# Linear attention, a Fourier mixer and an MLP on one core: k and q of the next chunk are turned between a chunk's output products and the turning back of that output

## The chip, the core and the metric

The kernel runs on one core of a Trainium2 chip. The core has a matrix engine (TensorE, PE in the profile; its weight loads are the row PEld), a vector engine (VectorE, DVE), a scalar engine (ScalarE, ACT), GpSimd (POOL) and SyncE (SP), which here issues DMAs only. Each engine works through its own list of instructions in order, and engines wait for each other by semaphores. The metric is device time in microseconds for one execution; the median of several runs counts.

## What is computed

A decayed linear attention over 4 batches, 8 heads, 768 positions and head size 64, then a mixer on rows of 512: the real part of a Fourier transform over positions and features is added, the sum is normalised, and an MLP of width 2048 is added to it.

```python
# attention, per block of 64 positions, with D[i,j] = lam**(i-j) for i >= j
out    = (q k^T * D) v + (q * lam**(i+1)) state
state  = lam**64 * state + (k * lam**(63-i))^T v
# mixer, on x = (batch, 768, 512)
u  = x + real(fft(fft(x, axis=1), axis=2))
un = (u - mean(u)) / sqrt(var(u) + 1e-6)
y  = u + maximum(un @ w_ch1, 0) @ w_ch2
```

The MLP's weights are given in float64, all else in float32; the computation is in float32.

## The kernel before

**Attention.** `attn_chunk(b, c)` does a chunk of 128 positions of batch b for all 8 heads, six chunks to a batch. SP loads k, q and v of the chunk (L243, two buffers each). GpSimd makes kd, the decayed k (L250, one buffer). PE turns k (L254, four 128x128 transposes) and q (L259, four more) into PSUM; ACT copies them out as kT (L256) and qT (L261); for c > 0 DVE makes the decayed qs from the same PSUM bank (L264). PE forms the scores (L272); DVE multiplies them by the decay in two halves (L276, called sc). PE forms the state's increment from kd and v (L287), which DVE adds (L292, or copies in the first chunk, L289) after GpSimd has decayed the old state (L291). The output is the sum of qs times the old state (L300) and sc times v (L304) in one PSUM bank. ACT copies it to oT (L307), PE turns it back (L311), ACT copies the result to x in two halves (L314, L315), and ACT's queue stores x to memory for the mirror (L318 to L322).

**Fourier part.** The transform uses that x can be folded with its own mirror image. `mirror_a` (called by chunk 4) and `mirror_b` (by chunk 5) read mirrored rows by GpSimd's indirect DMAs (L358, L361, L366). `fft_ln(b)` folds on DVE (L347 to L396, `fold_a` and `fold_b`), transforms over positions on PE (L420), over features (L433 to L438), and adds the result on ACT and DVE (L495 to L503). `norm` does the statistics (L450, L451), a power on GpSimd (L454, L455), and the scaling (L467); for the first four groups of rows PE turns the result (L472), for the others DVE does in squares of 32 (L477) and it waits in memory.

**MLP.** Weights come in 32 pieces (L209), which DVE and ACT unpack from float64 (L214 to L222). The first four groups of rows go through a plain MLP (L535, L549) while attention and transform of later batches run. The other eight go through `late`, seven products in place of eight (L617, L664), after all attention is done.

**What sets the order.** Each stage is a Python generator that yields its rough cost; `weave` and `part` take turns between attention and Fourier part of a batch on one side and weights or MLP on the other. From this order a scheduler makes the list of each engine; it keeps dependencies and buffers and may move an instruction forward or back by some places. PSUM for all but the plain MLP is one pool of five banks (`pa`).

The sections of a run are chosen by sums of costs, a chunk being 7.3:

```python
run(weave(attn(0), part(w, 0.5 * NW), 0.5 * NW / t_att))
run(weave(part(fr, t_chunk), part(w, 0.1 * NW), 0.1 * NW / t_chunk))
```

Of the kernel before, what the change touches and what calls it, by code (L numbers as in the profile page):

```python
# [76 lines left out]
def kernel(  # L77
# [15 lines left out]
    NC = S // C  # L93
# [45 lines left out]
    def new(pool, shape, tag, **kw):  # L139
        cnt[0] += 1  # L140
        return pool.tile(shape, F32, tag=tag, name=f"{tag}{cnt[0]}", **kw)

    def psum_a(shape):
        return new(pa, shape, "pa")
# [48 lines left out]
    def load_tables(i):  # L193
        if i == 1:
            nc.sync.dma_start(cs, cn["cs"].ap())
            nc.sync.dma_start(ix, cn["ix"].ap())
        elif i == 2:
            nc.sync.dma_start(dt, cn["dt"].ap())
# [37 lines left out]
    def pair(t, hp):  # L236
        return t[:, 2 * hp:2 * hp + 2, :].rearrange("p a d -> p (a d)")

    def attn_chunk(b, c):
        rows = slice(c * C, (c + 1) * C)  # L240
        kt, qt, vt = (new(ld, [C, H, D], nm) for nm in ("k", "q", "v"))
        for t, src in ((kt, k), (qt, q), (vt, v)):
            nc.sync.dma_start(t, src[b, :, rows, :].rearrange("h p d -> p h d"))  # L243
        if b == 0:
            load_tables(c)

        last = c == NC - 1
        if not last:
            kd = new(at, [C, H, D], "kd")
            nc.gpsimd.tensor_tensor(kd, kt, kpow, op=ALU.mult)  # L250

        ptk = psum_a([128, HP, C])
        for hp in range(HP):
            nc.tensor.transpose(ptk[:, hp, :], pair(kt, hp), ident)  # L254
        kT = new(at, [128, HP, C], "kT", bufs=2)
        nc.scalar.copy(kT, ptk)  # L256
        ptq = psum_a([128, HP, C])
        for hp in range(HP):
            nc.tensor.transpose(ptq[:, hp, :], pair(qt, hp), ident)  # L259
        qT = new(at, [128, HP, C], "qT", bufs=2)  # L260
        nc.scalar.copy(qT, ptq)  # L261
        if c > 0:
            qs = new(at, [128, HP, C], "qs")
            nc.vector.tensor_tensor(qs, ptq, qpow, op=ALU.mult)  # L264
        yield 1.2


        mm = nc.tensor.matmul
        pss = [psum_a([C, HP, C]) for _ in range(2)]
        for hp in range(HP):  # L270
            for hi in range(2):
                mm(pss[hi][:, hp, :], lhsT=kT[HD[hi], hp, :], rhs=qT[HD[hi], hp, :], start=True, stop=True)  # L272
        sc = []
        for hi in range(2):
            t = new(at, [C, HP, C], "sc", bufs=3)
            nc.vector.tensor_tensor(t, pss[hi], decay[:, hi::2, :], op=ALU.mult)  # L276
            sc.append(t)
        yield 1.5


        s_old, s_new = st[(c + 1) % 2], st[c % 2]
        if not last:
            pu = psum_a([128, HP, D])
            for hp in range(HP):
                for hi in range(2):
                    h = 2 * hp + hi
                    mm(pu[HD[hi], hp, :], lhsT=kd[:, h, :], rhs=vt[:, h, :], start=True, stop=True)  # L287
            if c == 0:
                nc.vector.tensor_copy(s_new, pu)  # L289
            else:  # L290
                nc.gpsimd.tensor_tensor(s_new, s_old, spow.broadcast_to([128, HP, D]), op=ALU.mult)  # L291
                nc.vector.tensor_tensor(s_new, s_new, pu, op=ALU.add)  # L292
            yield 0.9


        po = psum_a([128, HP, C])
        if c > 0:
            for hp in range(HP):
                for hi in range(2):
                    mm(po[HD[hi], hp, :], lhsT=s_old[HD[hi], hp, :], rhs=qs[HD[hi], hp, :],  # L300
                       start=(hp == 0), stop=False, skip_group_check=True)
        for hp in range(HP):
            for hi in range(2):
                mm(po[HD[hi], hp, :], lhsT=vt[:, 2 * hp + hi, :], rhs=sc[hi][:, hp, :],  # L304
                   start=(c == 0 and hp == 0), stop=(hp == HP - 1), skip_group_check=True)
        oT = new(at, [128, HP, C], "oT")
        nc.scalar.copy(oT, po)  # L307
        yield 2.0
        px = psum_a([C, HP, 128])
        for hp in range(HP):  # L310
            nc.tensor.transpose(px[:, hp, :], oT[:, hp, :], ident)  # L311
        px = px.rearrange("p h e -> p (h e)")
        x = xn_[b, c] = new(xp, [C, DM], "x") if c < HC else new(xn, [C, DM], "xn")
        nc.scalar.copy(x[:, 0:HM], px[:, 0:HM])  # L314
        nc.scalar.copy(x[:, HM:DM], px[:, DM - 1:HM - 1:-1])  # L315
        if c == 0:
            xd[b] = (dram.tile([S - 256, DM], F32, name=f"xa{b}"), dram.tile([257, DM], F32, name=f"xb{b}"))
            nc.scalar.dma_start(xd[b][1][256:257], x[0:1])  # L318
        elif c < NC - 1:
            nc.scalar.dma_start(xd[b][0][(c - 1) * C:c * C], x)  # L320
        if c >= NC - 2:
            nc.scalar.dma_start(xd[b][1][(c - NC + 2) * C:(c - NC + 3) * C], x)  # L322
        if c == NC - 2:
            mirror_a(b)
        elif c == NC - 1:
            mirror_b(b)
        yield 1.7
# [24 lines left out]
    def mirror_a(b):  # L352

        xa = xd[b][0]

        eo[b] = [(new(fp, [128, 2, 2 * W], f"fe{a}"), new(fp, [128, 2, 2 * W], f"fo{a}")) for a in range(2)]
        for a, n in enumerate(BLK):
            gather(out=eo[b][a][1][0:n, 1, 0:DM], out_offset=None, in_=xa[:, :], in_offset=row_of(a, n))  # L358
        for t in range(2, HC):
            u = xs[b, HC + t] = new(xp, [128, DM], "x")  # L360
            gather(out=u[:, :], out_offset=None, in_=xa[:, :], in_offset=row_of(2 + t))  # L361

    def mirror_b(b):
        for t in range(2):
            u = xs[b, HC + t] = new(xp, [128, DM], "x")
            gather(out=u[:, :], out_offset=None, in_=xd[b][1][:, :], in_offset=row_of(2 + t))  # L366
        for t in range(HC):
            xs[b, t] = xn_.pop((b, t))
# [325 lines left out]
            store(*who[1], y[1], lo if s == 0 else slice(0, DM))  # L694


    def attn(b):
        for c in range(NC):
            yield from attn_chunk(b, c)

    def front(b):
        yield from attn(b)
        yield from fft_ln(b)
# [32 lines left out]
    t_att, t_front = NC * t_chunk, NC * t_chunk + 10.0 + 7.0 + 5.7 + 3 * 2.4  # L736
    t_mlp = FO * 1.7 + G * 4 * 3.4
    run(weave(attn(0), part(w, 0.5 * NW), 0.5 * NW / t_att))

    fr, mix = chain(front(b) for b in range(1, B)), fft_ln(0)  # L740
# [58 lines left out]
```

## Time and profile before

| what | us |
|---|---|
| median of 5 runs | 867.81 |
| lowest and highest run | 866.45, 870.26 |
| the profiled execution, its own time | 871.22 |
| its span, first to last instruction | 869.4 |
| PE busy, matmuls | 808.2 |
| DVE busy | 438.5 |
| ACT busy | 177.1 |
| POOL busy | 85.0 |

The profile describes one execution, whose own time is 3.4 us over the median. The span is what its instructions cover; 1.8 us lie around it. PE's busy time is the sum of its matmuls with modelled ends, so 93% busy doesn't mean 93% of its peak. Where the prediction gives a wait in square brackets, it is the idle time of that engine just before the instruction, and whose result ended it. In the view of busy time by stage each row is a stretch of the span; the figure in round brackets is a count of instructions.

### The profile page before, as it was taken

To read this page: it belongs to the slowest core of one execution; us is meant where nothing else is said; L and a number is where in the kernel's file an instruction comes from. 1 tells how busy PE (TensorE), PEld (TensorE's weight loads), DVE (VectorE), ACT (ScalarE), POOL (GpSimd) and SP (SyncE) were. 2 spreads that over 40 slices of the span, in tenths; PEclk is the share of its full clock that TensorE was granted. 3 is DMA by queue.
4 is the path that set the end of the run, shared out by engine and by line. 5 is a ranking of instruction groups with operands and counts; after the bars stand their busy time and mean duration, and the time that the engine had idled before them with its cause. 6 is when DMAs were issued, how large, how long until landed. Compare 5 with 4: busy or idle time off the path is not lost.

```text
span 869.4 us, 11653 instructions
## 1 busy us (share of the span) xinstructions
PE 808.2 (93%) x4592; PEld 645.7 (74%) x4592; DVE 438.5 (50%) x1018; ACT 177.1 (20%) x417; POOL 85.0 (10%) x107
## 2 busy tenths in 40 slices
PE   5866768899999999999999999999999999999998
PEld 4655656645877477864874888888888888888887
DVE  6768869944552438426596553125511553035411
ACT  3453325510223112220200220012100220012100
POOL 2223211100021102111000000000000000000000
PEclk9985979999999999999999999999999999999999
DMA  9897516810156405542152101110111000110010
GB/s 247 207 254 209 143 57 172 261 45 25 49 124 132 140 25 141 103 109 79 48 169 51 49 1 49 48 49 1 49 46 45 7 1 1 48 49 1 1 37 24
DMA packets 127933, 71.63 MB, mean 82 GB/s; under 512 B 111336, under 2 KB 112360, under 8 KB 127880
## 3 DMA queue, kind: packets, MB, share of 16 engines
q1 hardware_dynamic: 121920, 56.72, 25.3%
q0 software_dynamic: 2496, 7.87, 2.8%
q10 hardware_dynamic: 3464, 6.30, 2.0%
q8 instruction: 36, 0.59, 0.3%
q14 instruction: 17, 0.14, 0.1%
HBM read 49.90 MB, written 20.98 MB: 82 GB/s over the span
## 4 chain that ended last, share of the span: by engine, by line
PE 75%; DVE 9%; DMA 7%; issue 5%; ACT 2%; POOL 1%; SPq 0%; ACTq 0%; POOLq 0%; DVEq 0%
PE p L664 22%; PE p L617 22%; PE pm L535 8%; PE pm L549 8%; DMA raw<-in_moe_w_ch_dram 4%; PE pa L420 3%; PE pa L304 3%; PE pa L272 2%; PE pa L300 2%; DMA fo<-xa,ix 1%; PE pa L311 1%; DMA x<-xb,ix 1%; PE pa L287 1%; DVE w L221 1%; PE pa L254 1%
## 5 line engine op out<-in xcount | busy, mean ns | idle before, releaser
L535 PE MATMUL pm<-ut,w 128*128 128x256 f32 x512 | 122.9, 389 | 4.3 <-ACT hr L543 4.3
L549 PE MATMUL pm<-w,hr 128*128 128x512 f32 x256 | 114.8, 596 | 0.0
L535 PEld LDWEIGHTS pm<-ut,w 128*128 128x128 f32 x512 | 95.1, 193 | 21.2 <-ACT hr L543 5.5
L617 PE MATMUL p<-ur,w 128*128 128x256 f32 x384 | 93.5, 379 | 0.0
L549 PEld LDWEIGHTS pm<-w,hr 128*128 128x128 f32 x256 | 47.0, 190 | 51.8 <-issue 51.2
L617 PEld LDWEIGHTS p<-ur,w 128*128 128x128 f32 x384 | 73.0, 190 | 10.3 <-issue 0.5
L617 PE MATMUL p<-us,w1s 128*128 128x256 f32 x256 | 65.5, 379 | 0.0
L664 PE MATMUL p<-w,hs 128*128 128x256 f32 x256 | 58.0, 379 | 0.5 <-DVE y L685 0.5
L664 PE MATMUL p<-w,ha 128*128 128x256 f32 x256 | 57.9, 379 | 0.0
L664 PE MATMUL p<-w2s,hs 128*128 128x256 f32 x256 | 57.9, 379 | 0.0
L664 PEld LDWEIGHTS p<-w,hs 128*128 128x128 f32 x256 | 48.5, 190 | 7.5 <-DVE y L685 0.9
L664 PEld LDWEIGHTS p<-w2s,hs 128*128 128x128 f32 x256 | 48.7, 190 | 6.6
L664 PEld LDWEIGHTS p<-w,ha 128*128 128x128 f32 x256 | 48.7, 190 | 6.6
L617 PEld LDWEIGHTS p<-us,w1s 128*128 128x128 f32 x256 | 48.7, 190 | 6.6
L525 POOL DMA_INDIRECT out_dram<-y,ix x12 | 11.8, 981 | 404.7 <-DVE y L690 344.1
L644 ACT COPY ha<-p 128x256 f32<-128x256 f32 x32 | 11.9, 372 | 170.8 <-PE p L617 170.8
L272 PE MATMUL pa<-qT,kT 64*128 64x128 f32 x384 | 32.1, 310 | 12.0 <-ACT qT L261 12.0
L272 PEld LDWEIGHTS pa<-qT,kT 64*128 64x128 f32 x384 | 26.9, 210 | 21.4 <-ACT qT L261 19.1
L304 PE MATMUL pa<-sc,v 128*64 128x128 f32 x384 | 33.1, 299 | 9.1 <-DVE sc L276 9.1
L264 DVE TENSOR_TENSOR qs<-pa,qpow 128x512 f32<-128x512 f32 x20 | 13.8, 689 | 48.4 <-ACT qT L261 48.4
L304 PEld LDWEIGHTS pa<-sc,v 128*64 128x64 f32 x384 | 24.7, 147 | 17.1 <-DVE sc L276 12.5
L655 DVE TENSOR_TENSOR ha<-p,ha 128x256 f32<-128x256 f32 x32 | 13.6, 425 | 44.2 <-ACT ha L654 44.2
(134 smaller groups left out, 1154.1 us busy)
## 6 DMA issues: line engine op xcount, KB each, us to landing
raw<-in_moe_w_ch_dram SPq DMA_DIRECT2D x32, 512.0 KB, 5.3
k<-in_k_dram SPq DMA_DIRECT2D x24, 256.0 KB, 5.1
q<-in_q_dram SPq DMA_DIRECT2D x24, 256.0 KB, 6.4
v<-in_v_dram SPq DMA_DIRECT2D x24, 256.0 KB, 3.8
ud<-x SPq DMA_DIRECT2D x16, 256.0 KB, 2.3
utd<-uq SPq DMA_DIRECT2D x64, 64.0 KB, 2.2
ur<-utd SPq DMA_DIRECT2D x8, 512.0 KB, 4.4
u<-ud SPq DMA_DIRECT2D x16, 256.0 KB, 2.7
```

The lines of the kernel that those rows point to most:

```text
L264: nc.vector.tensor_tensor(qs, ptq, qpow, op=ALU.mult)
L272: mm(pss[hi][:, hp, :], lhsT=kT[HD[hi], hp, :], rhs=qT[HD[hi], hp, :], start=True, stop=True)
L300: mm(po[HD[hi], hp, :], lhsT=s_old[HD[hi], hp, :], rhs=qs[HD[hi], hp, :], start=(hp == 0), stop=False, skip_group_check=True)
L304: mm(po[HD[hi], hp, :], lhsT=vt[:, 2 * hp + hi, :], rhs=sc[hi][:, hp, :], start=(c == 0 and hp == 0), stop=(hp == HP - 1), skip_group_chec ...
L420: mm = nc.tensor.matmul(ps[0:m, n, :], lhsT=piece(a, i, n), rhs=cs[0:rows, a, i in (2, 3), n, :], start=(a == 0), stop=(a == 1))
L525: nc.gpsimd.indirect_dma_start(out=out.rearrange("b s d -> (b s) d"), out_offset=row_of(2 + HC * (b + 1) + T - HC), in_=y[:, :], in_offset ...
L535: nc.tensor.matmul(ps, lhsT=w1[:, c, 128 * fc:128 * fc + 128], rhs=ut[:, c, :], start=(c == 0), stop=(c == KO - 1))
L549: nc.tensor.matmul(ps, lhsT=hr[fc // 4][:, fc % 4, 128 * i:128 * i + 128], rhs=w2[:, fc, :], start=(fc == 0), stop=(fc == FO - 1))
L617: nc.tensor.matmul(ps, lhsT=s2.A[a][:, kt, 128 * i:128 * i + 128], rhs=U[b][:, kt, :], start=(first and kt == 0), stop=(kt == 1), skip_gro ...
L644: nc.scalar.copy(a11, two(X))
L655: V.tensor_tensor(a22, two(Z), a22, op=ADD)
L664: nc.tensor.matmul(ps, lhsT=h[a][:, s, i, :], rhs=s2.B[b][:, i, :], start=(first and i == 0), stop=(i == HF - 1), skip_group_check=True)
```

## The change

`attn_chunk` is cut in two. `attn_in` loads a chunk, makes kd, turns k and q and copies them out. `attn_out` does all the rest. `attn` starts the first chunk's `attn_in` and then hands each `attn_out` the `attn_in` of the next chunk, which it runs to its end after the oT copy and in front of the turning back. The last chunk of a batch gets nothing to run, and the first chunk of the next batch starts as before. The sum of the yields stays the same; the 1.2 of a chunk's input part is yielded one chunk earlier. All buffers keep their sizes. Line numbers in the text are those of the kernel before.

```diff
-    def attn_chunk(b, c):
+    def attn(b):
+
+        head = attn_in(b, 0)
+        for c in range(NC):
+            yield from head
+            head = attn_in(b, c + 1) if c < NC - 1 else ()
+            yield from attn_out(b, c, head)
+
+    ins = {}
+
+    def attn_in(b, c):
         rows = slice(c * C, (c + 1) * C)
         kt, qt, vt = (new(ld, [C, H, D], nm) for nm in ("k", "q", "v"))
...
-        last = c == NC - 1
-        if not last:
+        kd = None
+        if c < NC - 1:
             kd = new(at, [C, H, D], "kd")
             nc.gpsimd.tensor_tensor(kd, kt, kpow, op=ALU.mult)
 
...
             nc.tensor.transpose(ptq[:, hp, :], pair(qt, hp), ident)
         qT = new(at, [128, HP, C], "qT", bufs=2)
         nc.scalar.copy(qT, ptq)
+        qs = None
         if c > 0:
             qs = new(at, [128, HP, C], "qs")
             nc.vector.tensor_tensor(qs, ptq, qpow, op=ALU.mult)
+        ins[b, c] = kT, qT, qs, kd, vt
         yield 1.2
+
+    def attn_out(b, c, head):
+        kT, qT, qs, kd, vt = ins.pop((b, c))
+        last = c == NC - 1
 
...
         oT = new(at, [128, HP, C], "oT")
         nc.scalar.copy(oT, po)
         yield 2.0
+        yield from head
         px = psum_a([C, HP, 128])
         for hp in range(HP):
             nc.tensor.transpose(px[:, hp, :], oT[:, hp, :], ident)
...
-    def attn(b):
-        for c in range(NC):
-            yield from attn_chunk(b, c)
-
     def front(b):
         yield from attn(b)
         yield from fft_ln(b)
```

## The prediction

> **What bounds the kernel now.** I read the page's slices first, then busy time by stage, then who PE waited for before 97 us, then one chunk boundary in order of time.
>
> ```profile
> span 869.4 us, 11653 instructions
> PE   5866768899999999999999999999999999999998
> DVE  6768869944552438426596553125511553035411
> PEclk9985979999999999999999999999999999999999
> DMA  9897516810156405542152101110111000110010
> ...
> core 0: us, PE busy (x) PEld busy (x) DVE busy (x) ACT busy (x) POOL busy (x), PEclk, DMA share, GB/s
> 0.00:25.00 25.00, 14.99 (x112) 12.39 (x114) 16.34 (x36) 8.28 (x14) 6.95 (x19) 1.00 0.99 245
> 25.00:60.00 35.00, 23.92 (x312) 19.35 (x308) 26.11 (x48) 17.80 (x35) 5.63 (x8) 0.99 0.86 227
> 60.00:97.00 37.00, 24.01 (x208) 20.35 (x210) 30.74 (x64) 12.06 (x25) 14.47 (x11) 0.64 0.65 188
> 97.00:121.00 24.00, 17.76 (x124) 15.05 (x120) 14.44 (x34) 9.08 (x22) 3.37 (x4) 0.79 0.42 132
> 121.00:177.00 56.00, 47.00 (x329) 38.02 (x329) 51.14 (x115) 28.84 (x57) 7.92 (x10) 0.97 0.60 176
> 177.00:449.00 272.00, 263.65 (x1654) 186.18 (x1654) 136.25 (x309) 52.69 (x137) 37.96 (x50) 1.00 0.36 89
> 449.00:869.00 420.00, 416.82 (x1867) 354.34 (x1865) 163.47 (x419) 48.37 (x129) 8.74 (x9) 1.00 0.11 32
> ...
> PE pa L272 <- ACT qT L261: 10.8, 9, 3.3
> PE pa L304 <- DVE sc L276: 7.7, 6, 3.8
> PE pa L311 <- ACT oT L307: 5.6, 8, 0.8
> PE pa L300 <- DVE qs L264: 5.1, 1, 5.1
> ...
> 33.65 0.58 ACT L307 COPY oT<-pa 128x512 f32<-128x512 f32 x1 [2.86 <-PE pa L304]
> 34.28 0.66 PE L311 MATMUL pa<-ident,oT 128*128 128x128 f32 x4 [0.68 <-ACT oT L307]
> 34.78 0.60 PE L254 MATMUL pa<-ident,k 128*128 128x128 f32 x4
> 35.21 0.60 PE L259 MATMUL pa<-ident,q 128*128 128x128 f32 x4
> 36.04 0.58 ACT L261 COPY qT<-pa 128x512 f32<-128x512 f32 x1
> 36.66 0.68 DVE L264 TENSOR_TENSOR qs<-pa,qpow 128x512 f32<-128x512 f32 x1
> 36.67 1.16 PE L272 MATMUL pa<-qT,kT 64*128 64x128 f32 x16 [0.86 <-ACT qT L261]
> ```
>
> From 177 us PE is the bound: 680.5 of 692 us busy, the last 420 us with no attention in them. Before that PE has 127.7 of 177 us of work and is idle for 49. Three things hold it there. To 60 us the DMA engines are nearly full (share 0.99, 0.86) and PE stops at every chunk boundary. From 60 to 97 us DVE (30.7 of 37) folds batch 0 for its transform. From 121 to 177 us DVE (51.1 of 56) unpacks the MLP weights, and PE's MLP waits behind it in DVE's order. So a microsecond saved on PE before 177 us counts only as far as it brings DVE to the weight work earlier; after 177 us it counts at once.
>
> **What the Trainium skill says.** "TensorE: Matmul & The Clock Gate", Part 2, step 1: weight loads can be pulled ahead, "The MATMULs themselves stay in program order". The boundary above agrees: k's transposes at 34.78, long ready, stand behind L311, which waits for oT. So their place in PE's order is the whole change. The same page, Part 1: the array runs at half clock until it has been busy for some microseconds. The trace agrees: four k transposes take 1.06 us at 18.1 us and 0.60 at 34.8. "PSUM — Partial Sum Buffer", on bank collisions: two engines may not touch one bank and quadrant together, so software must order them. The trace agrees: qs starts at 36.66, when ACT's qT copy of the same bank ends (36.62). "Trainium Kernel Development and Optimization", Key Constraints: the DMAs of SP, ACT and POOL share 16 engines. The trace fits: ACT issues chunk 4's rows at 51.27 and the gather that needs them begins at 59.91.
>
> **The change, step by step.** The built order has it as described: at all 20 boundaries inside a batch the eight transposes of L254 and L259 now stand behind the last L304 (a few start one product into L304) and in front of L311. The four boundaries between batches stay. No instruction is added or removed.
>
> *Step 1, to 60 us.* Before, after the last L304: the oT copy (0.58 us, PE idle 0.68), L311, L254, L259, then PE idle 0.86 for the qT copy. Now L254 and L259 take 0.87 us warm (34.78 to about 35.65), longer than the 0.63 from L304's end to L311's start, so the oT wait goes. ACT then runs oT, kT, qT (0.58, 0.59, 0.59 = 1.76, some 1.85 with hand-overs); PE reaches L272 after 0.87 + 0.50 (L311) = 1.37. What is late next is qT still, by about 0.45 warm and by nothing at half clock, where PE needs 2.6 us. Boundary by boundary in batch 0, by the brackets before L311 and L272: 0.68 + 0.67 = 1.35 (cold); 0.69 + 0.87 - 0.45 = 1.1; 0.68 + 0.86 - 0.45 = 1.1; 0.68 + 1.48 - 0.45 = 1.7; 0.80 + 1.38 - 0.45 = 1.7. Sum 7.0. In DVE's order chunk 5's two L276 also move in front of a weight piece whose data came at 55.84; that stop of L304 was 2.99. Together 9.9 us from PE's side.
> The DMA engines set the other bound. From 24 to 60 us they moved 8.05 MB. In 4 to 24 us, with full queues, the 4 us slices show 281, 276, 338, 235, 301 GB/s, mean 286; at that rate 8.05 MB take 28.1 us instead of 36. So at most 7.9 us can be had; nothing, if the small packets of k, q and v go no faster than now. I take 5.0, halfway on PE's side and well inside the DMA bound. SP's order is nearly unchanged (some k, q, v loads pass a weight piece), so no load is starved.
>
> *Step 2, 60 to 97 us.* DVE limits. Ahead of the end of fold_b its order now holds chunk 2's qs, both score products and the state add (0.69 + 2 x 0.68 + 0.41 = 2.46) and chunk 3's qs (0.69), less a weight piece's first two parts (0.43 + 0.69): 2.0 us more. But the transform (L420) started at 97.40, not at the fold's end at 94.6, because PE had chunk 2's L300 and L304 in between, stopped 5.07 by that qs. These now precede the fold's end: start at 94.6 + 2.0 = 96.6, 0.8 gained. DVE idles 4.2 us at 62 to 66 for the gather; batch 1's first score products and a weight piece now stand in front of that wait. Gain between 0 and 4.2; I take 1.5, since POOL's order takes some back: kd of batch 1's first chunk, in front of the mirror's gathers before, now stands behind three of them, for which POOL waited 9.9 us, and L287 on PE and L289 on DVE wait for kd. Last, the clock: L300 and L304 ran just before the transform and at 97 the clock was up again. Now PE may sit idle until the fold's first half is done, and begin the transform at half clock. Its five groups of eight L420 took about 1.5 us each warm, 7.5, and L433 to L438 some 1.9. Cost between 0 and 9.4; I take one 3.4 us stretch at half clock, as at 92 to 97 us, that is 1.7. Step 2: 0.8 + 1.5 - 1.7 = 0.6 gained.
>
> *Step 3, 97 to 121 us.* A chain of latency: transform, norm, transposes, with DVE idle 3.3 before the first L499 and 3.6 before the second. Two weight pieces move from in front of the first L499 to behind it (2 x 2.8 us: L215 0.43, L220 0.42, L221 0.69, L218 0.42, L222 0.69 and gaps). At the second L499 both orders have done the same DVE work, so nothing is won, and the norm's L450 and L467 can stand behind a piece's operation up to 0.7 us each. Cost 0 to 3; I take two of them, 1.4.
>
> *Step 4, 121 to 177 us.* The DVE work is the same, in nearly the same order, and 91% dense: the earlier start carries over.
>
> *Step 5, from 177 us.* PE is idle 8.4 us to 449 us, of which L311 0.7 and L304 0.9 can fall to this change. MLP products already cover the boundaries. Fewer of them now stand between L311 and L272, so qT can show by 0.1 to 0.45 at up to ten boundaries. Between 1.6 gained and 2 lost; I take 0.3 gained. The MLP work is the same in total, and round the transforms of batches 2 and 3 its amount barely differs.
>
> Sum: 5.0 + 0.6 - 1.4 + 0.3 = 4.5 us less. The profiled execution took 871.2 (span 869.4), so 866.7; the median of five is 867.8, so 863.3.
>
> **The rivals.** *Hidden:* the first 60 us are bound by DMA at today's rate and what PE saves is lost there. For: share 0.99, and weights awaited at 55.84. Against: DMA fell to 38 GB/s at 24 to 28 us, because v's load waited for PE's L304. Then only steps 2, 3 and 5 remain, -0.6 + 1.4 - 0.3 = 0.5 slower: 868.3.
>
> *More:* DMA reaches 286 GB/s, DVE fills all its wait for the gather and the clock holds: 7.9 + 0.8 + 4.2 - 1.4 + 0.3 = 11.8, less a third, since DVE at 83% can't take in all of it in step 2: 7.9, or 859.9. For: 9.9 on PE alone. Against: it needs three best cases.
>
> *Slower, by the clock:* the whole transform of batch 0 runs at half clock, 9.4 us longer instead of 1.7, with DVE waiting in L499 behind it: 4.5 - 7.7 = 3.2 slower, 871.0. It decides once more than 1.7 + 4.5 = 6.2 us of that warm work run at half clock. For: the granted clock was 0.50 from 60 to 80 us though PE was busy most of that time, so such a stretch can last; a PE idle for the fold goes into it. Against: at 92 to 97 us it lasted one short stretch, and L420 comes in a dense run.
>
> That the change doesn't take place is excluded by the built order.
>
> **How the numbers follow.** Forecast 0.47 (own range 860.5 to 866), hidden 0.15, more 0.16, slower 0.22. Less than 0.3% (2.6 us) can't be told from no change. Faster: 0.16 + 0.44 of the forecast = 0.60; same: 0.03 + 0.14 = 0.17; slower: 0.01 of hidden + 0.22 = 0.23. Range 856.5 to 870.5: it takes in most of "more", all of "hidden", and the nearer half of "slower".
>
> **What would show it.** Step 1: no wait of L311 for oT before 60 us, L272's below 0.5 a chunk, chunk 5's L304 ending near 55 instead of 59.8, and DMA above 250 GB/s there. Step 2: first L420 near 91 instead of 97.4, the clock back within 4 us of it, and no stop at L287 of batch 1's first chunk. Step 3: second L499 near 116. Step 4: the first long run of L549 near 173 instead of 177.5. From there to the end as before, within 1 us. I am wrong if chunk 5 still ends near 60, if the transform runs cold, or if PE's idle time after 177 grows by more than 2 us.

## The result and the profile after

The changed kernel takes 866.11 us (median of 42 runs, 862.5 to 874.72), the kernel before 868.96 us in the same sessions (79 runs). The ratio over all these runs is 0.9974, with a 95% interval (in square brackets behind a ratio from here on) of 0.9962 to 0.9986. Taken of 868.96 us, as all ratios below are, that is 2.3 us faster, by the interval 1.2 to 3.3; the medians alone lie 2.9 apart. The forecast was 4.5 us. The profiled execution after took 864.2 us, with a span of 862.3. That is 1.9 us under its median, and the one before, 871.2, is 2.3 us over the 868.96. So the two profiles differ by 7.0 us where the runs differ by 2.3, and what this one pair shows as gained is too much.

Line numbers have moved. L254 and L259 (k and q turned) are now L264 and L269, L261 (the qT copy) is L271, L272 is L288, L276 is L292, L304 is L320, L307 is L323 and L311 is L328. From L347 on, 17 is to be added: the transform L420 is L437, the plain MLP's products L535 and L549 are L552 and L566, `late` begins at L634 in place of L617.

The page's slices and the busy time by stage, in stretches that the prediction used:

```profile
span 862.3 us, 11642 instructions
PE   5877697899999799998999999999999999999998
PEclk9988799999999999999999999999999999999999
DMA  9998348200466115542244001110111000110010
```

```profile
core 0: us, PE busy (x) PEld busy (x) DVE busy (x) ACT busy (x) POOL busy (x), PEclk, DMA share, GB/s
0.00:25.00 25.00, 15.79 (x180) 12.73 (x182) 18.71 (x38) 10.99 (x20) 7.79 (x20) 1.00 0.98 243
25.00:60.00 35.00, 27.14 (x320) 21.71 (x318) 30.62 (x52) 19.99 (x38) 11.63 (x12) 0.90 1.08 283
60.00:97.00 37.00, 24.55 (x218) 19.72 (x216) 35.24 (x76) 15.04 (x33) 7.02 (x5) 0.90 0.72 193
...
177.00:449.00 272.00, 260.03 (x1642) 186.07 (x1641) 139.04 (x305) 51.26 (x134) 37.99 (x50) 0.99 0.38 93
```

In the slices, of 21.6 us each, PE is busier in the third and fourth (77 for 66), and DMA fuller in the second and fourth (9 and 8 for 8 and 7). Two rows of the stages answer the prediction. From 25 to 60 us the DMA engines moved 283 GB/s in place of 227, so what looked nearly full was not. SP's loads of k, q and v then waited for buffers that PE still read. Before, the largest group of such waits up to 60 us (in total, times, longest) was:

```profile
SPq L243 <- PE pa L304: 16.0, 5, 4.6
```

After, the waits for the same products (L320) are 0.5 us, though SP waits for other lines of PE (8.2 us for L288). That the earlier release of these buffers raised the rate fits this, but no run isolates it. And from 177 to 449 us PE is busy 260.0 of 272 us where it was busy 263.7: PE, the bound of this stretch, idles more than before.

The first part is seen at a chunk boundary of batch 0, in order of time, and in the view of who PE waited for up to 100 us (in total, times, longest):

```profile
26.79 0.66 PE L264 MATMUL pa<-ident,k 128*128 128x128 f32 x4
27.03 0.57 ACT L323 COPY oT<-pa 128x512 f32<-128x512 f32 x1
27.28 0.60 PE L269 MATMUL pa<-ident,q 128*128 128x128 f32 x4
27.49 0.59 ACT L266 COPY kT<-pa 128x512 f32<-128x512 f32 x1
27.72 0.60 PE L328 MATMUL pa<-ident,oT 128*128 128x128 f32 x4
27.97 0.60 ACT L271 COPY qT<-pa 128x512 f32<-128x512 f32 x1
28.62 1.16 PE L288 MATMUL pa<-qT,kT 64*128 64x128 f32 x16 [0.30 <-ACT qT L271]
```

```profile
PE pa L288 <- ACT qT L271: 5.7, 6, 3.4
PE pa L320 <- DVE sc L292: 5.3, 5, 2.2
...
PE pa L437 <- DVE fe L406: 2.8, 1, 2.8
...
PE pa L328 <- ACT oT L323: 1.4, 2, 0.7
```

k and q are turned while ACT copies oT, so L328 follows without a wait; the wait for qT is 0.30 us where it was 0.86. The waits for oT fell from 8 with 5.6 us to 2 with 1.4 us (the one at 47.1 us stands behind a batch's last chunk, which has nothing to run ahead), those for qT from 10.8 to 5.7 us. New is the wait of the first transform, L437, for the fold.

The second part is round the transform of batch 2. PE's own list before, from chunk 4's turning back (L311) to the transform, with GpSimd's first gather:

```profile
282.80 0.60 PE L311 MATMUL pa<-ident,oT 128*128 128x128 f32 x4
283.24 0.60 PE L254 MATMUL pa<-ident,k 128*128 128x128 f32 x4
283.67 0.60 PE L259 MATMUL pa<-ident,q 128*128 128x128 f32 x4
284.11 2.74 PE L549 MATMUL pm<-w,hr 128*128 128x512 f32 x6
...
288.26 1.12 POOL L358 DMA_INDIRECT fo<-xa,ix  x1 [6.50 <-DMA xb<-xn]
...
292.73 9.61 PE L549 MATMUL pm<-w,hr 128*128 128x512 f32 x22
304.17 0.90 PE L420 MATMUL pa<-cs,fe 128*128 128x193 f32 x4 [1.83 <-DVE fe L389]
304.90 1.02 PE L549 MATMUL pm<-w,hr 128*128 128x512 f32 x2
```

And after, with DVE and GpSimd in between:

```profile
270.85 0.60 PE L328 MATMUL pa<-ident,oT 128*128 128x128 f32 x4
271.29 1.02 PE L566 MATMUL pm<-w,hr 128*128 128x512 f32 x2
...
277.49 1.12 POOL L375 DMA_INDIRECT fo<-xa,ix  x1 [8.34 <-issue]
...
278.19 10.47 PE L566 MATMUL pm<-w,hr 128*128 128x512 f32 x24
...
281.19 0.69 DVE L364 TENSOR_TENSOR fe<-fo,xn 128x512 f32<-128x512 f32 x1 [6.47 <-DMA fo<-xa,ix]
...
286.74 0.94 POOL L383 DMA_INDIRECT x<-xb,ix  x1 [5.60 <-DVE y L573]
290.07 0.69 DVE L364 TENSOR_TENSOR fe<-x,x 128x512 f32<-128x512 f32 x1 [4.07 <-DMA x<-xb,ix]
...
293.44 1.24 PE L437 MATMUL pa<-cs,fe 128*128 128x193 f32 x4 [4.79 <-DVE fe L406]
294.48 1.91 PE L566 MATMUL pm<-w,hr 128*128 128x512 f32 x2
```

The transform hangs on a chain that begins at chunk 4's turning back: x is stored, gathered from xa (L375), folded (L364), DVE finishes one tile of the MLP's output in two halves behind that fold (L572, L573), which frees the slot for the gather from xb (L383), then the second fold. The chain takes 21.4 us before (282.80 to 304.17) and 22.6 after (270.85 to 293.44). The 1.2 us more lie between the turning back and the first gather (5.46 us before, 6.64 after), while x is on its way to memory; why that takes longer I have not isolated. PE has work to do meanwhile: 19.5 us of it before (21.4 less 1.83 idle), 17.8 after. Missing is the turning of chunk 5's k and q (0.87 us), which now stands in front of chunk 4's turning back. Missing are also two products of the MLP (30 in place of 32, 0.87 us); as 82 of these stand in front of the turning back in both kernels, the two now come behind the transform's start. 1.7 us less work and a chain 1.2 us longer make the idle time 4.79 us in place of 1.83. And the clock drops: L437 and L566 take 1.24 and 1.91 us where they took 0.90 and 1.02.

Below, T0 is the start of the first long product (first L549 before, L566 after), where PE becomes the bound. It came at 177.5 us before and at 163.2 after, 14.3 us earlier in this pair. One pair is not enough here: two kernels of the experiments below (b23 and c4only) have the order of PE, DVE, ACT and GpSimd up to T0 as before and reached it at 172.1 and 174.6 us, and six more profiles with the changed kernel's order up to there reached it at 164.0 to 167.7. The means, of three and of seven profiles, are 174.7 and 165.3, so the lead is nearer 9.4 us. From T0 to the start of `late` PE took 301.1 us before, 308.0 after. Busy time of PE alone, from T0 to batch 2's transform and from there to `late`, before and then after:

```profile
177.50:304.20 126.70, 121.64 (x752) 1.00 0.36 85
304.20:478.60 174.40, 171.11 (x974) 1.00 0.37 91
```

```profile
163.20:293.40 130.20, 122.07 (x749) 1.00 0.34 82
293.40:471.20 177.80, 173.96 (x976) 0.99 0.36 89
```

Idle time grew from 8.4 to 12.0 us, busy time from 292.8 to 296.0. Of these 3.3 us, 1.7 are half of the 3.4 us of half clock from 294.1 us on; 1.6 us more of busy time remain, which I have not traced further. In this pair 6.9 of the 14.3 us are so given back; `late` takes the same in both (391 us).

### The profile page after: what moved, and what is told of

Same layout as the page of the kernel before. It is cut to its first block, busy times and chain, and to the rows that moved or that the text cites. A ratio compares the mean times of both kernels' runs of the same rounds, so it can differ in the third digit from the quotient of the medians.

```text
span 862.3 us, 11642 instructions
## 1 busy us (share of the span) xinstructions
PE 805.2 (93%) x4592; PEld 640.6 (74%) x4592; DVE 442.7 (51%) x1018; ACT 178.9 (21%) x417; POOL 84.2 (10%) x107
## 4 chain that ended last, share of the span: by engine, by line
PE 73%; DVE 10%; DMA 7%; issue 6%; ACT 2%; POOL 1%; SPq 0%; POOLq 0%; DVEq 0%; ACTq 0%
PE p L681 22%; PE p L634 22%; PE pm L552 8%; PE pm L566 8%; DMA raw<-in_moe_w_ch_dram 4%; PE pa L437 3%; PE pa L320 2%; PE pa L288 2%; PE pa L316 1%; DMA x<-xb,ix 1%; DVE w L221 1%; DVE w L222 1%; PE pa L264 1%; DMA q<-in_q_dram 1%; DVE sc L292 1%
## 5 line engine op out<-in xcount | busy, mean ns | idle before, releaser
L552 PE MATMUL pm<-ut,w 128*128 128x256 f32 x512 | 121.4, 386 | 5.4 <-ACT hr L560 2.7
L566 PE MATMUL pm<-w,hr 128*128 128x512 f32 x256 | 114.8, 599 | 0.0
L552 PEld LDWEIGHTS pm<-ut,w 128*128 128x128 f32 x512 | 94.2, 191 | 21.9 <-ACT hr L560 3.7
L634 PE MATMUL p<-ur,w 128*128 128x256 f32 x384 | 93.7, 379 | 0.1
L566 PEld LDWEIGHTS pm<-w,hr 128*128 128x128 f32 x256 | 47.7, 191 | 53.2 <-issue 52.6
L634 PEld LDWEIGHTS p<-ur,w 128*128 128x128 f32 x384 | 72.9, 190 | 10.7 <-issue 0.5
L634 PE MATMUL p<-us,w1s 128*128 128x256 f32 x256 | 65.5, 379 | 0.0
L681 PE MATMUL p<-w2s,hs 128*128 128x256 f32 x256 | 57.9, 379 | 0.0
L681 PE MATMUL p<-w,ha 128*128 128x256 f32 x256 | 57.9, 379 | 0.0
L681 PEld LDWEIGHTS p<-w,hs 128*128 128x128 f32 x256 | 48.5, 190 | 7.5 <-DVE y L702 0.9
L634 PEld LDWEIGHTS p<-us,w1s 128*128 128x128 f32 x256 | 48.6, 190 | 6.6
L320 PE MATMUL pa<-sc,v 128*64 128x128 f32 x384 | 32.6, 292 | 6.9 <-DVE sc L292 6.8
L288 PE MATMUL pa<-qT,kT 64*128 64x128 f32 x384 | 32.1, 292 | 5.9 <-ACT qT L271 5.9
L288 PEld LDWEIGHTS pa<-qT,kT 64*128 64x128 f32 x384 | 27.2, 193 | 14.0 <-ACT qT L271 10.1
L292 DVE TENSOR_TENSOR sc<-pa,decay 128x512 f32<-128x512 f32 x48 | 31.5, 682 | 11.6 <-PE pa L288 11.5
L320 PEld LDWEIGHTS pa<-sc,v 128*64 128x64 f32 x384 | 24.0, 143 | 15.0 <-DVE sc L292 10.0
```

What stands on the lines that cost most here:

```text
L552: nc.tensor.matmul(ps, lhsT=w1[:, c, 128 * fc:128 * fc + 128], rhs=ut[:, c, :], start=(c == 0), stop=(c == KO - 1))
L566: nc.tensor.matmul(ps, lhsT=hr[fc // 4][:, fc % 4, 128 * i:128 * i + 128], rhs=w2[:, fc, :], start=(fc == 0), stop=(fc == FO - 1))
L634: nc.tensor.matmul(ps, lhsT=s2.A[a][:, kt, 128 * i:128 * i + 128], rhs=U[b][:, kt, :], start=(first and kt == 0), stop=(kt == 1), skip_gro ...
L681: nc.tensor.matmul(ps, lhsT=h[a][:, s, i, :], rhs=s2.B[b][:, i, :], start=(first and i == 0), stop=(i == HF - 1), skip_group_check=True)
```

## The experiments

Ten kernels, the changed one among them twice, were timed against the kernel before in three sessions (its medians there 870.64, 868.55, 867.42 us). Seven of them set for each boundary whether the next chunk's k and q are turned early, as in the change, or late, as before; in these the changed kernel's lines from L328 to L344 stand 2 further down, those behind 4: the transform is L441, the long product L570. Half clock is counted as the half of PE's busy time in the stretches where the trace's clock record shows 0.5.

**The new order in batches 0 and 1 alone, and in 2 and 3 alone.** My theory after the result, "chain": the gain comes ahead of T0, and the chain of batches 2 and 3 takes part of it back. Its rival, "own limit", is stated beside it.

```diff
         yield 2.0
-        yield from head
+        early = b < 2        # b01;  b >= 2 in b23
+        if early:
+            yield from head
...
+        if not early:
+            yield from head
```

> The new order in batches 0 and 1 alone; batches 2 and 3 as before. Theory (chain): the new order shortens the stretch up to the first long run of L549 by some 14 us, and gives about 6 back in batches 2 and 3, where MLP products and k's and q's transposes now run in front of chunk 4's turning back, on which the mirror's gathers wait. Then this kernel keeps the lead: first L549 run near 163 us, PE idle before batch 2's first L420 at most 2 us, ratio to before 0.988 to 0.993. Rival (own limit): what follows 177 us has a limit of its own and eats any early lead: ratio 0.996 to 0.999, as the whole change.

> The new order in batches 2 and 3 alone. Theory (chain): nothing gained early, first L549 run near 177 us as before, PE idle before batch 2's first L420 4 to 5 us instead of 1.8, ratio 1.003 to 1.008. Rival (own limit): no difference, 0.999 to 1.001.

The new order in batches 0 and 1 alone gave 0.9884 [0.9855, 0.9913], that in batches 2 and 3 alone 1.0065 [1.004, 1.009]: 10.1 us gained (7.6 to 12.6) and 5.6 us lost (3.5 to 7.8), together 4.5 us gained, beside 5.1 for the changed kernel in that session. From T0 to `late` the first takes 300.9 us, as before, and the second 306.9. T0 came at 166.1 us in the first (163 expected) and at 172.1 in the second (177 expected), within the spread above. So the loss belongs to the order in the last two batches, whatever lead there is.

**One boundary of those two batches in the old order, and that one alone in the new.** Chunk 4's turning back begins the chain, so only the boundary behind chunk 4 should matter.

```diff
-        early = b < 2
+        early = not (c == NC - 2 and b >= 2)     # c4old
+        early = c == NC - 2 and b >= 2           # c4only
```

> The whole change, but in batches 2 and 3 chunk 4 is turned back before chunk 5's k and q, as before the change. Theory (chain): the mirror's rows are stored earlier by those transposes and by MLP products, PE idle before batch 2's first L420 falls back to about 2 us and the half clock behind it goes; ratio 0.990 to 0.994. Rival (the whole order of batches 2 and 3 costs, not this boundary): as the whole change, 0.996 to 0.999.

> The old order everywhere but at the boundary from chunk 4 to chunk 5 of batches 2 and 3, two boundaries of twenty. Theory 'chain': these two carry the whole loss of the new order in batches 2 and 3: ratio 1.003 to 1.009; TensorE idle 4 to 6 us in front of batch 2's first L420 in place of 1.8, and 105.5 to 108.5 us from batch 2's first L420 to batch 3's in place of 104.5. Rival 'all five boundaries lose': two boundaries of ten give a fifth of the loss, ratio 0.999 to 1.002, idle in front of L420 below 2.5 us.

With that boundary of two batches in the old order: 0.9878 [0.9849, 0.9906], the lowest of all and below the 0.990 to 0.994 expected, and 301.4 us from T0 to `late`. With it alone in the new order: 1.0101 [1.0065, 1.0137]. The loss is a little larger than the chain's range in the expectation, the idle time at batch 2 a little smaller (3.81 us for at least 4), and batch 2's and batch 3's first transforms lie 108.9 us apart (at most 108.5 expected, 104.5 before). The rival, a fifth of the loss, is out. Who PE waited for from 177 to 449 us, the first line of that view in the changed kernel, in the one with the boundary old, and in the one with new order in batches 2 and 3 only:

```profile
PE pa L437 <- DVE fe L406: 8.8, 3, 4.8
```

```profile
PE pa L441 <- DVE fe L410: 4.2, 3, 1.8
```

```profile
PE pa L441 <- DVE fe L410: 8.0, 3, 4.4
```

4.2 us with a longest of 1.8 is to the tenth what the kernel before shows. In the kernel with the two boundaries alone:

```profile
302.51 1.66 PE L441 MATMUL pa<-cs,fe 128*128 128x193 f32 x4 [3.81 <-DVE fe L410]
303.96 1.92 PE L570 MATMUL pm<-w,hr 128*128 128x512 f32 x2
```

Two of twenty boundaries carry the loss: necessary by the first kernel, sufficient by the second. In the second 32 products of the MLP still stand behind the turning back, so only k's and q's turning is missing there (0.87 us), and the chain took 22.5 us, 1.1 longer; with the 1.83 us of before that is 3.8, as measured. At batch 3 it waited no longer than before (0.72 us for 0.98), so in this profile the wait grew at batch 2 alone. Over the profiles of all kernels without added products, the chain of batch 2 takes 21.0 to 21.4 us in the six with this boundary in the old order, and 22.2 to 23.8 in the five with it in the new.

**The changed kernel twice more**, in the sessions of the runs that it is compared with.

> The changed kernel again, beside the three others on one chip, for a second profile. Both theories: ratio 0.996 to 0.999; first L549 run 162 to 168 us.

> The changed kernel once more, as the measure for the kernel with the six added products: ratio 0.992 to 0.999, 308 to 311.5 us from T0 to the start of L617.

0.9941 [0.9917, 0.9966], below the range expected, and 0.9981 [0.9959, 1.0002]. From T0 to `late` 311.4 us (13.1 idle, 4.3 lost at half clock) and 307.0 us (11.0 and 1.7), the latter 1 us below what I had set for it.

**Where the early gain arises: batch 0 alone, batch 1 alone.**

```diff
-        early = b < 2
+        early = b == 0      # b0;  b == 1 in b1
```

> The new order in batch 0 alone, the old order in batches 1, 2 and 3. Theory 'early gain': what the change gains is gained in chunks 0 to 4 of batch 0, where TensorE has nothing but attention to do and stood idle at each boundary; in batch 1 the other batch's front covers the boundaries already. Then this kernel gains as much as the new order in batches 0 and 1 did: ratio 0.986 to 0.992, and the first long product of the MLP (T0) starts near 166 us as it did there. Rival 'each batch its share': batch 1 has the same five boundaries and gives about a third to a half of the gain; then the ratio here is 0.993 to 0.996 and T0 lies near 171 us.

> The new order in batch 1 alone. Theory 'early gain': nothing to be had there, ratio 0.998 to 1.002, T0 at the 177 us of the kernel before, within 2 us. Rival 'each batch its share': ratio 0.993 to 0.996 and T0 near 172 us.

Batch 0 alone: 0.9905 [0.9873, 0.9937], T0 at 165.5 us, as with both batches (0.9884, 166.1). Batch 1 alone: 0.9947 [0.9921, 0.9973], T0 at 170.2. So "early gain" is right for batch 0 and wrong for batch 1: alone, it brings 4.6 us (2.3 to 6.9), about half as much, but nothing that can be told on top of batch 0 (8.3 us gained with batch 0, 10.1 with both, and the intervals overlap). Up to T0 DVE is the busiest engine. Its busy time over three stretches (start to the end of batch 0's attention, to the first transform, to T0, as time, busy time, instructions, PE's clock, DMA share and GB/s), before and after:

```profile
0.00:59.80 59.80, 42.24 (x83) 1.00 0.91 234
59.80:97.40 37.60, 31.34 (x65) 0.64 0.65 187
97.40:177.50 80.10, 65.67 (x148) 0.91 0.54 163
```

```profile
0.00:46.40 46.40, 38.99 (x74) 1.00 1.02 259
46.40:78.60 32.20, 28.38 (x50) 0.84 0.96 264
78.60:163.20 84.60, 74.78 (x172) 0.92 0.57 161
```

Up to T0 DVE works 139.3 us before and 142.2 after; its idle time falls from 38.2 to 21.0 us. The first transform comes 18.8 us earlier, but 172 DVE instructions then lie between it and T0 in place of 148, and 4.5 us of the lead go there: up to T0 DVE has the same instructions in both but for one, and the transform now comes earlier among them. With the new order in batches 2 and 3 only, in batch 1, in batch 0 and in both of these DVE idles 34.3, 31.6, 24.9 and 24.6 us to T0, and with nearly the same work T0 follows it: 172.1, 170.2, 165.5, 166.1. The first of these has the old order up to T0, so differences of some 5 us between single profiles can be spread; the ratios carry the argument. Whether batch 1's share adds to that of batch 0 the intervals don't decide; with both, PE waits 3.1 us for the fold in front of the first transform, with one alone not at all.

**The boundary behind chunk 4 old in all four batches.**

```diff
-        early = b < 2
+        early = c != NC - 2
```

> The new order at every boundary but the one from chunk 4 to chunk 5, in all four batches. Theory 'chain' (the way from chunk 4's turning back through two gathers and two folds to the transform has a fixed length, and the work of chunk 5 that the new order puts in front of the turning back is missing behind it): in batches 2 and 3 as with the boundary of those batches alone in the old order; in batches 0 and 1 the idle time in front of the first L420 falls from 2.8 to 3.1 us towards 0 to 1.5 us, but the boundary's own wait of up to 1.7 us comes back: ratio 0.985 to 0.991, about the same as with batches 2 and 3 alone. Rival 'the early boundary counts in full': chunk 5 of batch 0 ends 1.7 us later and nothing comes back for it, ratio 0.990 to 0.994.

0.9901 [0.987, 0.9932]: it fits both. The idle time in front of the first transform stayed at 2.9 us, against what "chain" expected of the early batches; chunk 5 of batch 0 ended at 51.5 us in place of the 48.8 of the kernel with this boundary old in batches 2 and 3 alone, as the rival had it but more, yet T0 came at 166.3, 0.8 us later than there. Inconclusive on the early batches; behind T0 it is as without the loss (301.0 us to `late`).

**Filling the wait with products that nothing reads.** Is it the wait or the half clock behind it?

```diff
+        if last and b >= 2:        # dum_5_end, range(5);  b == 2 and range(6) in fill2
+            warm = psum_a([128, 512])
+            for i in range(5):
+                nc.tensor.matmul(warm, lhsT=ident, rhs=ident[:, 0:1].broadcast_to([128, 512]), start=True, stop=True)
```

> The whole change, and behind chunk 5's turning back in batches 2 and 3 five products of the identity with a row of 512 that nothing reads (about 0.25 us each, work that the kernel doesn't need). They shorten TensorE's idle stretch in front of the first L420 without moving the chain that it waits for. Theory 'latency': the loss at batch 2's transform is the wait for the fold; the products fill it and bring nothing: the ratio stays that of the changed kernel, 0.992 to 0.999, with no change of the first L420's place. Rival 'half clock': [...]the 3.4 us of half clock after it are a good part of the loss; then L437 and L566 behind the wait keep 0.90 and 1.02 us in place of 1.24 and 1.91, and the ratio is 2 to 3 us better, 0.989 to 0.993.

> The whole change, and behind chunk 5's turning back of batch 2 alone six products of the identity with a row of 512 that nothing reads: 0.45 us each by the run before, 2.7 us together, less than the 4.8 to 6.0 us that TensorE stood idle there. Theory 'half clock': the idle stretch falls to 2 to 3 us, the clock stays up, and the 1.7 to 2.9 us that the changed kernel lost at half clock between 177 us and the start of L617 come back: 305 to 307 us from T0 to L617 in place of 308.0 and 311.4, ratio 0.002 to 0.005 below that of the changed kernel in the same call. Rival 'latency alone': the products only take the place of idle time, 308 to 311 us, ratio as that of the changed kernel, within 0.002.

The products were larger than I had reckoned: each is two records of 0.445 us, 4.5 us in each batch of the first kernel and 5.3 us in the second, both about as much as the idle time they were to fill. The first gave 0.9996 [0.9976, 1.0017], outside both ranges expected, the second 0.9975 [0.9959, 0.9992] beside 0.9981 for the changed kernel. In the second the clock held (L347 are the added products; one line of DVE is shown with PE's):

```profile
280.02 5.34 PE L347 MATMUL pa<-ident 128*128 128x512 f32 x12
285.20 10.46 PE L570 MATMUL pm<-w,hr 128*128 128x512 f32 x24
...
288.83 0.42 DVE L576 TENSOR_TENSOR y<-pm,x 128x256 f32<-128x256 f32 x1 [1.44 <-PE pm L570]
...
297.13 0.90 PE L441 MATMUL pa<-cs,fe 128*128 128x193 f32 x4 [1.47 <-DVE fe L410]
297.87 1.02 PE L570 MATMUL pm<-w,hr 128*128 128x512 f32 x2
```

L441 and L570 are back at 0.90 and 1.02 us, and no half clock is left between T0 and `late`. From T0 to `late` it took 306.7 us where the changed kernel of the same session took 307.0: 3.7 us less idle and 1.7 less lost at half clock, against some 5.2 more of busy time for the products. The half clock is real and cost 1.7 us in that session's changed kernel, but products of this size cost what they save, so the pair doesn't decide by its totals. Nor did they leave the chain where it was, as the expectation had it: they stand in front of the MLP products that DVE's tile of output needs, so this tile, which frees the gather's slot, waits 1.44 us for PE (1.02 in the first kernel, none in the changed one), and the chain grows from 22.4 to 24.4 us. By the profiles the wait is the larger part in two of three (3.6 and 2.7 us more idle than before, with 1.7 of half clock in each), and in the third they are near each other (4.8 and 4.3).

## Why the prediction came out as it did

The direction was right, the size twice what was measured. It was the sum of two errors against each other: up to T0 the change brings more than twice as much as forecast (10.1 us by the kernel with the new order in the first two batches only, for 4.2), and behind T0 it takes back 5.6 us where the forecast had next to nothing. That even the direction held is luck in part: the forecast's early gain with the measured loss would have been 1.4 us slower.

**Step 5 is the step that failed.** It said that "round the transforms of batches 2 and 3 its amount barely differs" and took 0.3 us gained. Measured are 6.9 us lost between T0 and `late` in the profile (3.6 idle, 1.7 half clock, 1.6 more busy), and 5.6 us by the kernel with the new order in those batches only. The amount of work does differ by little, 1.7 us. But the transform already waited 1.83 us for its fold, so each microsecond taken from behind chunk 4's turning back counted at once, and so did the 1.2 us by which the chain itself grew. The step asked which part of PE's 8.4 us of idle time could fall, and priced the chunk boundaries, where MLP products do cover; it did not ask what the moved transposes had covered in their old place. The last sentence of the prediction named the sign: PE's idle time after 177 us grew by more than 2 us.

**Step 1, mis-sized.** 5.0 us were taken, from 9.9 on PE's side and 7.9 by the DMA engines. Chunk 5's last L304 ended at 46.4 us, not near 55. Of the 13.4 us, some are not the order: in two kernels with the old order in batch 0 and the clock up from 15.0 and 13.5 us on in place of 25.2, it ended at 55.3 and 57.9 us. Against these the order is worth 8.9 and 11.5 us (to 46.4, the clock up from 14.2 us). PE's side was nearly sound. Over the five boundaries of batch 0 the waits before L311 and L272 fell from 8.8 to 1.1 us (7.7 for the 7.0 reckoned; qT was 0.24 to 0.30 us late in four for the 0.45 reckoned), and the 2.99 us of chunk 5's L304 went. But "no load is starved" was wrong once:

```profile
35.92 0.63 PE L269 MATMUL pa<-ident,q 128*128 128x128 f32 x4 [2.07 <-DMA q<-in_q_dram]
```

That leaves 8.6 us. The bound of 7.9 by the DMA engines was none. The rate that it drew on was reached (283 GB/s for 286), but it took the same bytes to be moved up to the end of chunk 5. By the rows shown above 14.0 MB were moved up to there before (59.8 us at 234 GB/s) and 12.0 after (46.4 us at 259). So the choice of 5.0 was too low, and the case in which the packets go no faster than before did not come.

**Steps 2 to 4.** The first transform came at 78.6 us, not near 91: from chunk 5 to it 5.4 us less than before, for 0.6, though L287 of batch 1's first chunk did stop for kd, by 1.59 us. The second L499 came at 104.6 us, not near 116: from the transform to it 3.6 us more, for 1.4. From there to T0 it took 0.9 us more, for none. Together 0.9 gained in place of 0.8 lost, so these steps hold as a sum, by luck, and not one by one. "At the second L499 both orders have done the same DVE work" was right (174 instructions up to it in both, 80 of them on weights), and yet time was lost ahead of it. That DVE sets T0, and that a microsecond of PE counts there only through DVE, fits DVE's times above; no run tests it. T0 was forecast at 173 and came at 163.2, at 165.3 in the mean of the seven profiles.

**The rivals.** "Hidden" fell with the 283 GB/s. "More", 7.9 us gained, is nearer to the early stage (10.1) than the forecast, but had no loss behind. "Slower by the clock" did take place once: in the changed kernel's second profile the clock was at half from 76.2 to 96.7 us, all through batch 0's transform, and T0 came at 167.7 us in place of 163.2; in the other two it was back after 3.4 us, as step 2 had it. Even then T0 lay 4.4 to 9.8 us ahead of the three profiles with the old order, as the early lead was larger than forecast.

A kernel that beats both came out of it: leave the boundary behind chunk 4 of the last two batches in the old order (0.9878), or use the new order in batches 0 and 1 only (0.9884). The two can't be told apart.

## What to carry to other kernels

Work that is moved forward leaves a gap where it was: before pricing it as free, find the longest chain that starts behind the new place, and count what is left to cover that chain. If a wait on that chain shows already, however short, there is no slack in the cover. A DMA share near 0.9 was no bound here, where the transfers waited for buffers that a stalled engine held: compare the rate with that of a stretch with full queues, and ask whether all bytes have to come before the moment that is timed. And two profiles with the same order can differ by as much as a change is worth: T0 spread over 5.4 us with the old order up to it, over 4.5 with the new.

## What was unexpected of the hardware

The first time the clock came up differed by kernel more than by run: at 14.2, 14.8 and 14.6 us in three profiles of the changed kernel, at 19.5 to 20.4 us in six variants with the new order in batch 0 (one profile each), at 13.5, 15.0, 24.6 and 25.2 us in four kernels with the old. Coming up at 20.3 us rather than 14.6, batch 0's attention ended 2.0 us later (48.5 and 46.5 us). What sets it I don't know.

"TensorE: Matmul & The Clock Gate" in the Trainium skill, Part 1, has the clock drop after an idle window of about 3.4 us. The trace agrees for the idle stretch of 4.79 us, behind which the clock was at half for 3.4 us. But shorter ones sufficed: 2.84 us ahead of batch 0's transform (half from 79.0 us on, with other short waits before it), and at batch 3's transform 2.7 us in the changed kernel's second profile, where 2.5 us in the first did not. So, once here, 3.4 us at half clock came with a wait of 2.7 us.
